# Attention into a mixture of experts on one core: the order of the first two units, identity matmuls in a pause, and W2's buffers

## The chip, the core and the metric

The kernel runs on one core of a Trainium2 chip. Its engines each have an instruction queue of their own: PE (TensorE, matmuls), PEld (its weight loads), DVE (VectorE), ACT (ScalarE), POOL (GpSimd) and SP (SyncE, whose queue issues nearly all DMAs). The metric is device time of one execution in microseconds. Working memory is SBUF; matmuls write to PSUM, of which the kernel uses four double buffers, all called `dbl`.

## What is computed

Eight batches of 576 tokens and eight heads of 64 columns go through two attentions: 32 summary queries `p` per head attend to k and v, and the tokens `q` attend to the result. The tokens' output then goes through four experts with the weights of `domain_probs`. Shapes: q, k, v 8x8x576x64, p 8x8x32x64, w1 4x512x1024, w2 4x1024x512, all float32.

```python
def _attn_ref(q, k, v, p):
    scale = 1.0 / np.sqrt(q.shape[-1])
    def sm_attn(qq, kk, vv):
        s = scale * np.matmul(qq, kk.transpose(0, 1, 3, 2))
        s = s - np.max(s, axis=-1, keepdims=True)
        a = np.exp(s)
        a = a / (np.sum(a, axis=-1, keepdims=True) + 1e-09)
        return np.matmul(a, vv)
    p_packed = sm_attn(p, k, v)
    return sm_attn(q, p_packed, p_packed)

def _moe_ref(x, domain_probs, w1, w2):
    p = domain_probs / (domain_probs.sum(-1, keepdims=True) + 1e-09)
    out = np.zeros((N, D), dtype=np.float32)
    for e in range(E):
        h = np.maximum(x @ w1[e], 0.0)
        out += p[:, e:e + 1] * (h @ w2[e])
    return out
```

## The kernel before

**Units.** The experts' hidden width, 4 x 1024, is cut into eight blocks `ch` of 512. A unit is one block for one batch; the batches come in four pairs (super-blocks `sb`), and the first units are (block 0, batch 0), (block 1, batch 0), (block 1, batch 1), (block 0, batch 1). What follows speaks of units 0 and 1 above all, both of batch 0, and of unit 2, which is the first of batch 1.

**Attention.** `pack_unit` makes the packed summaries `ppbd` for one batch and one group g of four heads. `tok_unit` makes the tokens' probabilities against the 32 summaries: transposes of the scores (`a`), row maximum m2, a-m, exp on ACT, row sum s2, its inverse, a x s, a transpose back (`at`), and a split of `at` into a high part `xh` (ACT cast) and the rest `xl` (POOL subtraction), so that the product of float32 values can be done in three matmuls of a shorter type. `tok_halves` does this for batch 0 in two halves of 288 tokens, c = 0 and 1: `turned`, `shifted`, `normed`.

**First product.** `g_form` multiplies the summaries by W1 (raw tiles `wraw`) into `ghl`, high and low part. `mm1_group(u, kh, c)` multiplies `ghl` by `xh`/`xl` in 24 matmuls of 288 columns, for half kh of the block and half c of the tokens. DVE then applies relu and the token's weight (`pbt`) in one SCALAR_TENSOR_TENSOR. The four results are the quarters a11, a21, a12, a22 of a matrix.

**Second product.** It is done as a seven-product scheme (Strassen and Winograd): operands a11, a12, a22 and s1 to s4 (sums of quarters, tiles `sblk`, `ablk`) against the corresponding t of W2. `s_operand` splits an operand into `st`, high part on ACT, low part on POOL. `t_form` does the same for W2 (raw tiles `rw0`, `rw1`) into `tt`, and forms t1 to t4 by four subtractions. `product(u, i)` is 12 matmuls of 288 columns, in the sequence ORDER = a11, s3, s1, s2, a22, s4, a12; its result is copied or added to `acc`. At the end of a batch pair `combine` adds the accumulators and stores them.

**What sets the order.** The program is recorded by a helper, and a scheduler then places each engine's instructions by their dependences. Wrappers add order edges: `InOrder` (`vq` for DVE, `gq` for POOL) keeps an engine in the order of the program while `.on` is set; `Behind` (`avec`, `cvec`, `bact`, `bpool`) puts an instruction behind the last one that another wrapper noted. `vec` and `vacc` note DVE's operand sums and accumulations. So all of DVE's and POOL's instructions made through a wrapper appear in the profile under one line, 68. Background attention for batch 1 is a generator, `back`, two steps of which are taken after each product of unit 0.

Of the kernel before, what the change touches and what calls it, by code (L numbers as in the profile page):

```python
# [16 lines left out]
P = 128  # L17
# [16 lines left out]

ORDER = ["a11", "s3", "s1", "s2", "a22", "s4", "a12"]
NPROD = len(ORDER)


@with_exitstack
def attention_moe(ctx: ExitStack, tc: tile.TileContext, q, k, v, p, dp, w1, w2, out):  # L40
# [262 lines left out]
    def tok_halves(b, new):  # L303
        xs[b] = tuple(xpool.tile([P, NG, 2, HP], F32R, name=f"{n}{b // 2 % 2}") for n in ("xh", "xl"))
        qts = []
        for g in range(NG):
            qts.append(new[g](b, [P, 2, S], "qt"))
            nc.sync.dma_start(out=qts[g], in_=q[b][:, 2 * g:2 * g + 2, :])
        yield
        pss = [  # L310
            scores([b], g, lambda b, pr, hh: ppbd[b % 4][hh * D:(hh + 1) * D, pr, :], {b: qts[g]})[b]
            for g in range(NG)
        ]
        yield
        n = HS // 32
        a2s = [new[g](b, [P, 2 * n, NPK], "a1") for g in range(NG)]
        ats = [new[g](b, [P, S], "at") for g in range(NG)]
        def block(g, c):
            return a2s[g][:, c * n:(c + 1) * n]

        def turned(g, c):
            vq.transpose(out=block(g, c).rearrange("p a n -> p (a n)"), in_=pss[g][:, c, 0:HS])

        def shifted(g, c):
            a2 = block(g, c)
            m2 = small.tile([P, n, 1], F32, name="m2")
            vq.tensor_reduce(out=m2, in_=a2, axis=AX.X, op=ALU.max)
            vq.tensor_tensor(out=a2, in0=a2, in1=m2.broadcast_to([P, n, NPK]), op=ALU.subtract)
            nc.scalar.activation(out=a2, in_=a2, func=AF.Exp, scale=SCALE)

        def normed(g, c):
            a2, ts = block(g, c), slice(c * HS, (c + 1) * HS)
            s2 = small.tile([P, n, 1], F32, name="s2")
            vq.tensor_reduce(out=s2, in_=a2, axis=AX.X, op=ALU.add)
            vq.tensor_scalar_add(s2, s2, 1e-9)
            vq.reciprocal(out=s2, in_=s2)
            vq.tensor_tensor(out=a2, in0=a2, in1=s2.broadcast_to([P, n, NPK]), op=ALU.mult)
            vq.transpose(out=ats[g][:, ts], in_=a2.rearrange("p a n -> p (a n)"))
            xh, xl = (t[:, g, c, 0:HS] for t in xs[b])
            hi_of(xh, ats[g][:, ts], nc.scalar)  # L340
            lo_of(xl, ats[g][:, ts], xh, gq)

        for g in range(NG):
            turned(g, 0)
            shifted(g, 0)
        yield
        normed(0, 0)
        for g in range(NG):
            turned(g, 1)
        normed(1, 0)  # L350
        yield
        for g in range(NG):
            shifted(g, 1)
        yield
        for g in range(NG):
            normed(g, 1)
        yield

    def w1_load(ch):
# [10 lines left out]
    def g_form(bs, ch, raws, late=False):  # L370

        pss, calls = {}, []
        for g in range(NG):
            ps = dbl()
            for hs in range(4):
                pr, hh = 2 * g + hs // 2, hs % 2
                rows = slice(hh * D, (hh + 1) * D)
                for b in bs:
                    pss[g, b] = ps[:, b % 2]
                    c0 = (hs // 2) * 2 * NPK + cols(b, hh).start  # L380
                    calls.append(dict(
                        out=pss[g, b][c0:c0 + NPK, :], lhsT=ppbd[b % 4][rows, pr, :], rhs=raws[pr][rows, :],
                        start=True, stop=True,
                    ))
        together(calls)
        for g in range(NG):
            for b in bs:
                ghl = gpool.tile([P, 2, FC], F32R, name="ghl", bufs=6)
                hi_of(ghl[:, 0, :], pss[g, b], nc.scalar)
                if not late:  # L390
                    lo_of(ghl[:, 1, :], pss[g, b], ghl[:, 0, :], vq)
                gs.setdefault((b, ch), []).append(ghl)
            if not late:
                yield
        if late:
            yield
            for g in range(NG):
                for b in bs:
                    ghl = gs[b, ch][g]
                    lo_of(ghl[:, 1, :], pss[g, b], ghl[:, 0, :], vq)  # L400
            yield

    units = [(0, 0, 0), (0, 1, 0), (0, 1, 1), (0, 0, 1)]
# [6 lines left out]
        pbt[b] = t  # L410

    blocks = {}

    def mm1_group(u, kh, c):
        sb, ch, b = units[u]
# [22 lines left out]
        def add(dst, x, y, op):  # L438
            vec.tensor_tensor(out=dst, in0=x, in1=y, op=op)

        name = f"a{c + 1}{kh + 1}"
        vec.scalar_tensor_tensor(
            out=held(name) if c == kh else psv, in0=psv, scalar=0.0,
            in1=pbt[b][:, ts].rearrange("p (o t) -> p o t", o=1).broadcast_to([P, 2, HS]),
            op0=ALU.max, op1=ALU.mult,
        )
        if name == "a21":
            add(held("s3"), blocks[u, "a11"], psv, ALU.subtract)
            add(psv, psv, blocks[u, "a22"], ALU.add)
            add(held("s2"), psv, blocks[u, "a11"], ALU.subtract)  # L450
            nc.scalar.copy(out=held("s1"), in_=psv)  # L451
            if (u, "a12") in blocks:
                add(held("s4"), blocks[u, "a12"], blocks[u, "s2"], ALU.subtract)
        elif name == "a12":
            if (u, "s2") in blocks:
                add(held("s4"), psv, blocks[u, "s2"], ALU.subtract)
            else:
                blocks[u, "a12"] = psv
            st = hpool.tile([P, 2, 2, HP], F32R, name="stl")[:, :, :, 0:HS]
            hi_of(st[:, 0], psv, nc.scalar)  # L460
            lo_of(st[:, 1], psv, st[:, 0], vec)
            blocks[u, "op", NPROD - 1] = st

# [29 lines left out]
    def raw_tile(shape, name):  # L493
        return wpool.tile(shape, F32, name=name)

    def t_form(ch, first=False):

        raw = [w2r.pop((ch, kh)) for kh in range(2)]
        blk = {
# [4 lines left out]
        steps = (  # L504
            ("a11", "t1", "t3"), ("s3", "s1", "t2"), ("s2", "t4"), ("a22",), ("s4",), ("a12",),
        )
        how = {"t1": ("b12", "b11", "b11"), "t2": ("b22", "t1", "t1"), "t3": ("b22", "b12", "b12"), "t4": ("t2", "b21", "t2")}
        for names in steps:
            for name in names:
# [5 lines left out]
            for name in names:  # L515
                if name in how:
                    x, y, place = how[name]
                    bpool.tensor_tensor(out=blk[place], in0=blk[x], in1=blk[y], op=ALU.subtract)
                    blk[name] = blk[place]
                else:  # L520
                    t = tt[ch, ORDER.index(name)]
                    lo_of(t[:, 1], blk[of[name]], t[:, 0], bpool)
# [116 lines left out]
    with ExitStack() as first:  # L639
# [42 lines left out]
            next(gen)  # L682
        next(halves)
        drain(fold)
        next(halves)
        next(forms)
        mm1_group(0, 0, 0)
        s_operand(0, 0)
        next(halves)
        mm1_group(0, 1, 0)  # L690
        for gen in packs[2:]:
            next(gen)
        mm1_group(0, 1, 1)
        mm1_group(0, 0, 1)
        s_operand(0, 1)
        vq.on = gq.on = False
        drain(forms)

    apool = ctx.enter_context(tc.tile_pool(name="apool", bufs=2, reuse_waits="tile"))
# [13 lines left out]
    GROUPS = {1: ((0, 0),), 3: ((1, 1),), 4: ((0, 1),), 6: ((1, 0),)}  # L713
    GROUPS_FIRST = {2: ((0, 0),), 3: ((1, 1),), 4: ((0, 1),), 6: ((1, 0),)}
    GROUPS_LATE = {3: ((0, 0),), 4: ((1, 1),), 5: ((0, 1),), 6: ((1, 0),)}
    FORM = {0: (0, 2, 3, 4, 5, 6), 2: (6,), 3: (0, 1, 2, 3, 4)}
    for kh in range(2):
        w2_load(1, kh, raw_tile)
    tsteps = nothing
    kind = None  # L720
    sums, back = nothing, second_batch()
    for u, (sb, ch, b) in enumerate(units):
        pos = u % (2 * NCH)
        odd = pos % 2 == 1
        opening = u < 4
        nxt = units[u + 1] if u + 1 < len(units) else None

        if u == 1:
            drain(back)
            avec.on = cvec.on = bact.on = bpool.on = order["strict"] = True  # L730
        if sb + 1 < SB and pos == (2 if sb == 0 else 1):
            drain(back)
            back, kind = pair_attention([2 * sb + 2, 2 * sb + 3]), None
# [1 line left out]
        gsteps, gat = nothing, (0, 1)  # L735
        nsb, nch = (sb, ch + 1) if ch + 1 < NCH else (sb + 1, 0)
        if u == 0:
            gsteps, gat = g_form([0], 1, raws), (0,)
        elif u == 1:
            gsteps, gat = g_form([1], 1, raws), (0,)  # L740
        elif u == 2:
            gsteps, gat = g_form([1], 0, raws), (0,)
        elif u > 2 and not odd and nsb < SB:
            gsteps = g_form([2 * nsb, 2 * nsb + 1], nch, raws)
        fch = {0: 1, 2: 2, 3: 2}.get(u, ch + 1 if u > 3 and sb == 0 and ch + 1 < NCH else None)
        if fch is not None and u != 3 and not (u > 3 and odd):
            tsteps = t_form(fch)
        form_at = FORM.get(u, () if fch is None else (1, 2, 3, 4) if odd else (1, 4))
        for i in range(NPROD):
            product(u, i)  # L750
# [3 lines left out]
            elif nxt:  # L754
                s_operand(u + 1, n - NPROD)
            if i in gat:
                if gat == (0,):
                    drain(gsteps)
                    if 0 < u < 4:
                        raws = w1_load({1: 0, 2: 2}[u])  # L760
# [6 lines left out]
                    mm1_group(u + 1, *grp)  # L767
            if i == 4 and 2 <= u < len(units) - 2 and units[u + 2][1] % 2 == 0:
                load_probs(units[u + 2][2], units[u + 2][1] // 2)
            if u == 0:  # L770
                next(back, None)
                next(back, None)
            elif i == 5 and kind != "scores" or i == 2 and u > 2 or i == 0 and odd and u > 3:
                kind = next(back, None)
            if i in form_at:
                next(tsteps, None)
            if u == 1 and i < 2:
                w2_load(2, i, raw_tile)
# [51 lines left out]
```

## Time and profile before

| | before |
|---|---|
| median of 3 runs | 1281.56 us (1281.49 to 1284.88) |
| profiled execution | 1281.34 us, span 1279.6 us |
| mean granted TensorE clock | 0.995 |
| PE busy | 1245.8 us, 97% of the span |
| DVE, ACT, POOL busy | 934.1, 498.2, 734.8 us |
| chain that ended last | PE 90%, DVE 4%, DMA 2%, POOL 2% |

The rows of the timeline read: start in us, duration, engine, line of the program, operation, output tile <- input tiles, shapes, count; the bracket at the end is the idle time of the engine just before, and the instruction that ended it. `[5.68 <-POOL xl L68]` on a PE row means that PE stood still for 5.68 us until POOL had written `xl`. Rows of the waits read: engine and tile, what it waited for, total us, times, longest. Instructions follow each other slightly sooner than their durations say, since the next begins while the last one drains.

### The profile page before, as it was taken

What the parts mean: (1) busy time and instruction counts of PE and PEld (TensorE: products, weight loads), DVE (VectorE), ACT (ScalarE), POOL (GpSimd) and SP (SyncE); (2) the same over time, 40 slices, a digit from 0 to 9 for tenths busy, and PEclk for the clock granted to TensorE, in tenths of its full rate; (3) what the DMA queues carried; (4) which work ended last, traced back from release to release, by engine and by line L of the source; (5) the groups of instructions that cost most, each with busy time, mean ns of one, the idle gap of its engine ahead of it and who ended that gap; (6) DMA issues with size and microseconds to landing.
All of it is one profiled execution on the core that took longest, in us unless ns stands there. A gap on an engine that the chain in (4) does not pass through costs nothing.

```text
span 1279.6 us, 26886 instructions
## 1 busy us (share of the span) xinstructions
PE 1245.8 (97%) x10720; PEld 1165.0 (91%) x10720; DVE 934.1 (73%) x1398; ACT 498.2 (39%) x850; POOL 734.8 (57%) x528
## 2 busy tenths in 40 slices
PE   6899999999999999999999999999999999999996
PEld 3789899999999999999998999999999999999996
DVE  6676676888875677889776667788968466776667
ACT  3554544444445333334325434233334523332331
POOL 3876978798674434455566434454448544544554
PEclk9999999999999999999999999999999999999999
DMA  9765565545556444464444465433346443434322
GB/s 340 253 249 191 208 234 197 193 142 170 182 181 223 155 164 150 140 195 158 136 161 157 158 206 176 152 116 127 118 158 213 154 134 119 132 116 155 125 66 75
DMA packets 86219, 213.71 MB, mean 167 GB/s; under 512 B 8784, under 2 KB 27344, under 8 KB 86096
## 3 DMA queue, kind: packets, MB, share of 16 engines
q1 hardware_dynamic: 85424, 211.85, 49.6%
q8 instruction: 86, 1.41, 0.5%
q14 instruction: 37, 0.30, 0.1%
q10 hardware_dynamic: 672, 0.15, 0.1%
HBM read 173.09 MB, written 38.87 MB: 166 GB/s over the span
## 4 chain that ended last, share of the span: by engine, by line
PE 90%; DVE 4%; DMA 2%; POOL 2%; ACT 1%; issue 1%; DVEq 0%; SPq 0%; POOLq 0%; ACTq 0%
PE dbl L116 84%; PE dbl L124 5%; DVE acc L68 2%; DMA pnd<-ablk 1%; POOL st L68 1%; PE dbl L119 1%; DMA pbt<-pnd 1%; DVE a L68 1%; DVE sblk L68 0%; POOL tt L68 0%; DMA wraw<-in_w 0%; DVE dbl L68 0%; DVE ghl L68 0%; DMA rw<-in_w 0%; ACT st L151 0%
## 5 line engine op out<-in xcount | busy, mean ns | idle before, releaser
L116 PE MATMUL dbl<-st,tt 128*128 128x288 f32 x4608 | 666.4, 296 | 8.9 <-DVE ghl L68 5.1
L116 PEld LDWEIGHTS dbl<-st,tt 128*128 128x128 f32 x4608 | 623.1, 188 | 44.8 <-POOL st L68 24.8
L68 POOL TENSOR_TENSOR st<-sblk,st 128x576 fp32r<-128x576 f32 x256 | 370.0, 1456 | 447.4 <-ACT st L151 446.1
L116 PE MATMUL dbl<-xh,ghl 128*128 128x288 f32 x2048 | 413.6, 294 | 0.0
L68 DVE TENSOR_TENSOR acc<-dbl,acc 128x576 f32<-128x576 f32 x391 | 293.5, 752 | 87.9 <-PE dbl L116 85.5
L116 PEld LDWEIGHTS dbl<-xh,ghl 128*128 128x128 f32 x2048 | 328.2, 188 | 0.2 <-DVE ghl L68 0.2
L151 ACT CAST st<-sblk 128x576 fp32r<-128x576 f32 x256 | 166.7, 675 | 368.6 <-DVE sblk L68 296.7
L116 PE MATMUL dbl<-xl,ghl 128*128 128x288 f32 x1024 | 302.9, 296 | 6.0 <-POOL xl L68 5.7
L68 POOL TENSOR_TENSOR st<-ablk,st 128x576 fp32r<-128x576 f32 x128 | 188.6, 1473 | 45.4 <-ACT st L151 45.3
L116 PEld LDWEIGHTS dbl<-xl,ghl 128*128 128x128 f32 x1024 | 192.7, 188 | 8.8 <-POOL xl L68 6.4
L68 DVE SCALAR_TENSOR_TENSOR dbl<-dbl,pbt 128x576 f32<-128x576 f32 x128 | 97.8, 764 | 80.4 <-PE dbl L116 79.2
L68 DVE SCALAR_TENSOR_TENSOR ablk<-dbl,pbt 128x576 f32<-128x576 f32 x128 | 96.4, 753 | 67.7 <-PE dbl L116 65.2
L151 ACT CAST st<-ablk 128x576 fp32r<-128x576 f32 x128 | 86.3, 674 | 126.7 <-PE dbl L116 93.8
L116 PE MATMUL dbl<-stl,tt 128*128 128x288 f32 x768 | 113.0, 296 | 0.0
L116 PEld LDWEIGHTS dbl<-stl,tt 128*128 128x128 f32 x768 | 104.4, 188 | 0.2
L68 DVE TENSOR_TENSOR ghl<-dbl,ghl 128x512 fp32r<-128x512 f32 x128 | 84.9, 685 | 23.6 <-ACT ghl L151 23.6
L151 ACT CAST ghl<-dbl 128x512 fp32r<-128x512 f32 x128 | 72.3, 590 | 55.8 <-DVE ghl L68 54.8
L68 POOL TENSOR_TENSOR tt<-rw,tt 128x512 fp32r<-128x512 f32 x56 | 72.7, 1315 | 18.6 <-ACT tt L85 18.6
L68 DVE TENSOR_TENSOR stl<-dbl,stl 128x576 fp32r<-128x576 f32 x64 | 48.4, 756 | 39.1 <-ACT stl L151 39.1
L124 PE MATMUL dbl<-wraw,ppbd 64*32 64x512 f32 x1024 | 67.6, 595 | 0.9 <-DMA wraw<-in_w 0.9
L451 ACT COPY sblk<-dbl 128x576 f32<-128x576 f32 x64 | 41.1, 642 | 65.6 <-DVE sblk L68 65.6
L544 ACT COPY acc<-dbl 128x576 f32<-128x576 f32 x56 | 35.9, 642 | 51.8 <-PE dbl L116 49.1
(63 smaller groups left out, 703.4 us busy)
## 6 DMA issues: line engine op xcount, KB each, us to landing
tt<-td SPq DMA_DIRECT2D x175, 512.0 KB, 4.1
wraw<-in_w SPq DMA_DIRECT2D x132, 256.0 KB, 4.3
td<-tt SPq DMA_DIRECT2D x56, 512.0 KB, 5.2
pbt<-pnd SPq DMA_DIRECT2D x32, 288.0 KB, 3.8
out<-acc SPq DMA_DIRECT2D x32, 288.0 KB, 2.7
rw<-in_w SPq DMA_DIRECT2D x16, 512.0 KB, 5.7
kt<-in_k SPq DMA_DIRECT2D x14, 576.0 KB, 5.6
kt<-in_q SPq DMA_DIRECT2D x14, 576.0 KB, 5.4
```

The lines of the kernel that those rows point to most:

```text
L68: res = getattr(self.eng, op)(*args, **kw)
L116: on_pe(nc.tensor.matmul(**kw))
L119: on_pe(nc.tensor.transpose(**kw))
L124: ins = nc.tensor.matmul(**kw).ins
L151: return eng.copy(out=dst, in_=src)
L451: nc.scalar.copy(out=held("s1"), in_=psv)
L544: nc.scalar.copy(out=accs[b, i], in_=psv)
```

## The change

It moves work in the first 90 us and, with it, the places of some later instructions:

- In `tok_halves` the normalisation of the second half's group 0 comes a step sooner; DVE does it ahead of a11's SCALAR_TENSOR_TENSOR.
- `warm(16)` issues 16 matmuls of `ident` with itself, between the first-half and the second-half groups of unit 0.
- a12 of unit 0 is held in SBUF and split as the other operands are, by ACT and POOL (`early`), instead of from PSUM by ACT and DVE (`stl`).
- The operands 1 to 3 of unit 0 are formed in a loop at once, POOL's `gq` stays in order through unit 0, and the wrappers' `on` flags are set before unit 0, not before unit 1.
- In unit 0 `t_form(1)` makes its subtractions by `avec` (DVE), not by `bpool` (POOL), at other positions (FORM); `g_form` follows product 1, not product 0; of `back`, two steps follow each of the first five products of unit 0 and the first two of unit 1.
- Block 1's W2 goes into two buffers of `xpool` named `xh1`, not into `rw0` and `rw1`.
- `g_form`'s low parts are made through `vec`.

```diff
@@ tok_halves
         for g in range(NG):
             shifted(g, 1)
+        normed(0, 1)
         yield
-        for g in range(NG):
-            normed(g, 1)
+        normed(1, 1)
         yield
@@ g_form (twice)
-                    lo_of(ghl[:, 1, :], pss[g, b], ghl[:, 0, :], vq)
+                    lo_of(ghl[:, 1, :], pss[g, b], ghl[:, 0, :], vec)
@@ new
+    def warm(n):
+        ps = dbl()
+        together([
+            dict(out=ps[:, 0, 0:P], lhsT=ident, rhs=ident, start=True, stop=True) for _ in range(n)
+        ])
@@ mm1_group
+        early = name == "a12" and (u, "a22") not in blocks
         vec.scalar_tensor_tensor(
-            out=held(name) if c == kh else psv, in0=psv, scalar=0.0,
+            out=held(name) if c == kh or early else psv, in0=psv, scalar=0.0,
...
-            else:
-                blocks[u, "a12"] = psv
+            if early:
+                return
             st = hpool.tile([P, 2, 2, HP], F32R, name="stl")[:, :, :, 0:HS]
@@ t_form
-    def t_form(ch, first=False):
+    def t_form(ch, first=False, eng=bpool):
...
+        if first:
+            steps = steps[:1] + (("s3", "s1"), ("t2",)) + steps[2:]
...
-                    bpool.tensor_tensor(out=blk[place], in0=blk[x], in1=blk[y], op=ALU.subtract)
+                    eng.tensor_tensor(out=blk[place], in0=blk[x], in1=blk[y], op=ALU.subtract)
@@ the opening
         drain(fold)
+        next(forms)
         next(halves)
         next(forms)
         mm1_group(0, 0, 0)
+        next(halves)
         s_operand(0, 0)
-        next(halves)
         mm1_group(0, 1, 0)
+        next(forms)
+        warm(WARM)
         for gen in packs[2:]:
             next(gen)
         mm1_group(0, 1, 1)
         mm1_group(0, 0, 1)
-        s_operand(0, 1)
-        vq.on = gq.on = False
+        for i in range(1, 4):
+            s_operand(0, i)
+        avec.on = cvec.on = bact.on = bpool.on = order["strict"] = True
+        order["product"] = order["free"][-1]
+        vq.on = False
         drain(forms)
@@ the units
-    FORM = {0: (0, 2, 3, 4, 5, 6), 2: (6,), 3: (0, 1, 2, 3, 4)}
+    FORM = {0: (3, 3, 4, 5, 6, 6), 2: (6,), 3: (0, 1, 2, 3, 4)}
     for kh in range(2):
-        w2_load(1, kh, raw_tile)
+        w2_load(1, kh, lambda shape, name: xpool.tile(shape, F32, name="xh1"))
...
+        gq.on = u == 0
-        if u == 1:
-            drain(back)
-            avec.on = cvec.on = bact.on = bpool.on = order["strict"] = True
...
-            gsteps, gat = g_form([0], 1, raws), (0,)
+            gsteps, gat = g_form([0], 1, raws), (1,)
...
-            tsteps = t_form(fch)
+            tsteps = t_form(fch, eng=bpool if u else avec)
...
-            if u == 0:
-                next(back, None)
-                next(back, None)
+            if u < 2:
+                for _ in range(2 if i < 5 - 3 * u else 0):
+                    next(back, None)
```

In what follows a row gives line, operation, output <- inputs and columns; the number behind a name tells buffers apart.

POOL, from t1 of block 1 to s3 of unit 1. In before `rw0` and `rw1` hold block 1's W2; `st` from sblk_830 is s3, from sblk_835 s1, from sblk_833 s2, from ablk_770 a22, and `xl0` from at_918 is batch 1's.

```order
L68 TENSOR_TENSOR tt_796<-rw0_557,tt_796 128x512
L68 TENSOR_TENSOR rw0_557<-rw0_557,rw1_559 128x2x256
L68 TENSOR_TENSOR tt_845<-rw0_557,tt_845 128x512
L68 TENSOR_TENSOR tt_877<-rw1_559,tt_877 128x512
L68 TENSOR_TENSOR tt_926<-rw1_559,tt_926 128x512
L68 TENSOR_TENSOR st_896<-sblk_830,st_896 128x2x288
L68 TENSOR_TENSOR st_944<-sblk_835,st_944 128x2x288
L68 TENSOR_TENSOR st_988<-sblk_833,st_988 128x2x288
L68 TENSOR_TENSOR st_1008<-ablk_770,st_1008 128x2x288
L68 TENSOR_TENSOR xl0_375<-at_918,xh0_374 128x2x288
```

The same place in after, where `xh1_578` and `xh1_580` hold block 1's W2, ablk_482 is a12 of unit 0, ablk_731 a11 of unit 1, sblk_849 s1, sblk_847 s2 and sblk_844 s3:

```order
L69 TENSOR_TENSOR tt_804<-xh1_578,tt_804 128x512
L69 TENSOR_TENSOR tt_806<-xh1_578,tt_806 128x512
L69 TENSOR_TENSOR st_827<-ablk_482,st_827 128x2x288
L69 TENSOR_TENSOR tt_859<-xh1_578,tt_859 128x512
L69 TENSOR_TENSOR st_879<-ablk_731,st_879 128x2x288
L69 TENSOR_TENSOR st_944<-sblk_849,st_944 128x2x288
L69 TENSOR_TENSOR st_998<-sblk_847,st_998 128x2x288
L69 TENSOR_TENSOR tt_882<-xh1_578,tt_882 128x512
L69 TENSOR_TENSOR st_901<-sblk_844,st_901 128x2x288
```

The subtractions of W2 are gone from POOL, a12's split has come, and s3's (st_901) stands behind s1's and s2's; batch 1's `xl0` follows five instructions later.

DVE, around a21 of unit 1 (dbl_816 in before). a1_781 and a1_793 are the attention tiles of batch 1, one for each head group, m2 and s2 their row maxima and sums.

```order
L68 SCALAR_TENSOR_TENSOR ablk_770<-dbl_757,pbt_313 128x576
L68 STREAM_TRANSPOSE a1_781<-dbl_772 128x288 x2
L68 TENSOR_REDUCE m2_837<-a1_781 128x18
L68 STREAM_TRANSPOSE a1_793<-dbl_784 128x288 x2
L68 TENSOR_TENSOR a1_781<-a1_781,m2_837 128x576
L68 TENSOR_REDUCE m2_841<-a1_793 128x18
L68 TENSOR_TENSOR a1_793<-a1_793,m2_841 128x576
L68 SCALAR_TENSOR_TENSOR dbl_816<-dbl_816,pbt_313 128x2x288
L68 TENSOR_REDUCE s2_867<-a1_781 128x18
```

In after, with dbl_830 for a21 and a1_784 and a1_796 for the attention tiles:

```order
L69 SCALAR_TENSOR_TENSOR ablk_773<-dbl_760,pbt_313 128x576
L69 TENSOR_TENSOR xh1_578<-xh1_578 128x2x256
L69 STREAM_TRANSPOSE a1_784<-dbl_775 128x288 x2
L69 TENSOR_TENSOR xh1_578<-xh1_580,xh1_578 128x2x256
L69 STREAM_TRANSPOSE a1_796<-dbl_787 128x288 x2
L69 SCALAR_TENSOR_TENSOR dbl_830<-dbl_830,pbt_313 128x2x288
L69 TENSOR_TENSOR xh1_578<-xh1_580,xh1_578 128x2x256
L69 TENSOR_TENSOR sblk_844<-ablk_731,dbl_830 128x576
L69 TENSOR_TENSOR dbl_830<-dbl_830,ablk_773 128x2x288
L69 TENSOR_TENSOR sblk_847<-dbl_830,ablk_731 128x576
L69 TENSOR_REDUCE m2_851<-a1_784 128x18
L69 TENSOR_REDUCE m2_855<-a1_796 128x18
```

The maxima and a-m of batch 1 have moved behind a21's product and the sums of quarters, and W2's subtractions have come in between.

DVE at the end of the first super-block, where `combine` (acc_1263, acc_1164 are accumulators) meets `g_form`'s low parts:

```order
L68 TENSOR_TENSOR stl<-dbl,stl 128x2x288
L68 TENSOR_TENSOR acc_1263<-acc_1263,acc_1164 128x576
L68 TENSOR_TENSOR ghl<-dbl,ghl 128x512 x3
L68 SCALAR_TENSOR_TENSOR ablk<-dbl,pbt 128x576
L68 TENSOR_TENSOR acc_1208<-acc_1208,acc_1263 128x576
```

```order
L69 TENSOR_TENSOR stl<-dbl,stl 128x2x288
L69 TENSOR_TENSOR ghl<-dbl,ghl 128x512 x2
L69 TENSOR_TENSOR acc_1281<-acc_1281,acc_1182 128x576
L69 TENSOR_TENSOR ghl<-dbl,ghl 128x512
L69 SCALAR_TENSOR_TENSOR ablk<-dbl,pbt 128x576
```

Two of the three `ghl` now stand ahead of the accumulators' addition. The same holds at the ends of the second and the third super-block.

More of the change, by code (lines that the diff above doesn't have):

```diff
@@ L36 @@
 NPROD = len(ORDER)
+WARM = 16
 @with_exitstack
@@ L399, in g_form @@
                     ghl = gs[b, ch][g]
-                    lo_of(ghl[:, 1, :], pss[g, b], ghl[:, 0, :], vq)
+                    lo_of(ghl[:, 1, :], pss[g, b], ghl[:, 0, :], vec)
             yield
@@ L756, in attention_moe @@
             if i in gat:
-                if gat == (0,):
+                if len(gat) == 1:
                     drain(gsteps)
@@ L769, in attention_moe @@
                 load_probs(units[u + 2][2], units[u + 2][1] // 2)
-            if u == 0:
-                next(back, None)
-                next(back, None)
+            if u < 2:
+                for _ in range(2 if i < 5 - 3 * u else 0):
+                    next(back, None)
             elif i == 5 and kind != "scores" or i == 2 and u > 2 or i == 0 and odd and u > 3:
                 kind = next(back, None)
-            if i in form_at:
+            for _ in range(form_at.count(i)):
                 next(tsteps, None)
```

## The prediction

> **What bounds the kernel now.** I read the page first: one engine is nearly always busy.
>
> ```profile
> PE 1245.8 (97%) x10720; PEld 1165.0 (91%) x10720; DVE 934.1 (73%) x1398; ACT 498.2 (39%) x850; POOL 734.8 (57%) x528
> ```
>
> The span is 1279.6 us, so all that this change can save is in PE's waits, and any new wait of PE is a loss. The view of the waits, for 0 to 80 us and for the rest, ranks them (total, times, longest):
>
> ```profile
> PE dbl L116 <- POOL xl L68: 5.7, 1, 5.7
> ...
> PE dbl L116 <- DVE ghl L68: 5.1, 4, 1.3
> ```
>
> The first is one pause near 30 us; the second is met four times later. The timeline shows the pause:
>
> ```profile
> 26.77 0.46 DVE L68 TENSOR_TENSOR a<-a,m 128x288 f32<-128x288 f32 x1
> 28.16 0.76 DVE L68 SCALAR_TENSOR_TENSOR ablk<-dbl,pbt 128x576 f32<-128x576 f32 x1 [0.94 <-DMA pbt<-pnd]
> 31.29 0.48 DVE L68 STREAM_TRANSPOSE at<-a 128x288 f32<-128x288 f32 x1
> 33.42 0.48 DVE L68 STREAM_TRANSPOSE at<-a 128x288 f32<-128x288 f32 x1
> 34.09 0.61 PE L116 MATMUL dbl<-xl,ghl 128*128 128x288 f32 x1 [5.68 <-POOL xl L68]
> 34.44 0.80 POOL L68 TENSOR_TENSOR xl<-at,xh 128x288 fp32r<-128x288 f32 x1 [0.40 <-ACT xh L151]
> 39.60 1.75 PE L116 MATMUL dbl<-st,tt 128*128 128x288 f32 x12
> ...
> 43.67 1.31 PE L119 MATMUL dbl<-ident,a 128*128 128x128 f32 x10 [0.48 <-ACT sblk L451]
> ```
>
> PE waits 5.68 us because `xh`/`xl` of the second token half do not exist; DVE first does a11's product with the probabilities (28.16), then both heads' normalisation. The view by windows gives the granted clock (us, busy PE, PEld, DVE, ACT, POOL, then PEclk, DMA share, GB/s):
>
> ```profile
> 28.00:30.00 2.00, 0.41 (x4) 0.18 (x2) 1.73 (x5) 0.67 (x1) 1.92 (x3) 1.00 1.02 382
> 30.00:32.00 2.00, 0.00 (x0) 0.00 (x0) 1.97 (x3) 0.20 (x1) 2.00 (x2) 0.82 1.10 369
> 32.00:34.00 2.00, 0.00 (x0) 0.00 (x0) 1.86 (x6) 0.30 (x2) 2.00 (x3) 0.50 1.02 391
> ...
> 38.00:40.00 2.00, 2.00 (x16) 2.00 (x16) 1.29 (x5) 1.62 (x4) 1.32 (x2) 0.98 0.71 289
> ```
>
> PE stopped 0.41 us into the first window, at 28.4. 0.82 means half clock from 31.28 on, 0.98 that it ended near 38.1. The 24 matmuls between 34.09 and 39.60 took 5.51 us.
>
> **The change part by part.** The later boundaries come first, since they stand alone; then I walk both programs along PE, comparing when the same matmuls start.
>
> *The later boundaries.*
>
> ```profile
> 366.78 1.82 DVE L68 TENSOR_TENSOR acc<-acc,acc 128x576 f32<-128x576 f32 x1
> 368.53 0.68 DVE L68 TENSOR_TENSOR ghl<-dbl,ghl 128x512 fp32r<-128x512 f32 x1
> ...
> 370.81 2.47 PE L116 MATMUL dbl<-st,tt 128*128 128x288 f32 x17 [1.29 <-DVE ghl L68]
> ...
> 988.28 3.40 PE L116 MATMUL dbl<-st,tt 128*128 128x288 f32 x24 [1.30 <-DVE ghl L68]
> ```
>
> At three ends of a super-block, of which the first and the last are shown, a 1.82 us addition stands ahead of the `ghl` that PE waits for. In after two `ghl` stand ahead of it; they start 1.75 sooner than at 368.53, more than the 1.29 that PE waited: **-3.9** for three, at worst 0.
>
> *Leg 1, the pause.* DVE now goes from 26.77 straight to g0's normalisation (start 27.2). In before that chain ran from 28.9 to the end of the transpose, 31.77, so 2.9 us: it ends at 30.1 to 30.4 now. Then a11's product, 0.7, to about 31.1; then g1's chain, 2.1 (31.77 to 33.90): 33.3 to 33.8. ACT's cast and POOL's `xl` ended 1.34 behind the transpose in before (35.24 against 33.90): 34.6 to 35.2. The second head's part is needed by the fourth matmul, so 24 matmuls at full clock (0.131 each by the 39.60 row, 1.75 less the last one's 0.30 over 11; 3.15) end at 37.3 to 38.0 against 39.60: 1.6 to 2.3 ahead. a11's own operand follows 2.2 later, with its cast and POOL's part done by 35, still ahead of product(0,0).
>
> The 16 identity matmuls need a free PSUM buffer, which a11's product releases; by the order they start at 31.1, not 28.4. The nearest row is the transposes' against the same `ident`, 0.131 each: 2.1 us, at half clock 4.2. They stand ahead of matmuls that cannot start before 34.2, so only the half-clock end costs anything (up to 1). The nearest row for the clock is before's own: the step down came at 31.28 behind a stretch that held under half a microsecond of PE work. After leaves the same stretch (27.9 to 31.3) nearly as empty: 28.4 to 31.1 is 2.7 us of idleness. The drop therefore can still come, but the identity matmuls fill the next stretch, so it ends about 34.7. I put one such stretch at 0 to 1.7 us (24 matmuls at half clock for part of it), take 0.9, and two at 3.3. [...]
>
> *Leg 2, to 50 us.* The group of 16 `wraw` matmuls moves behind product(0,1), which so comes sooner. But the next lock is the second `at` copy:
>
> ```profile
> 44.74 1.83 PE L116 MATMUL dbl<-st,tt 128*128 128x288 f32 x12
> 47.72 0.74 ACT L85 COPY at<-dbl 128x512 f32<-128x512 f32 x2
> 48.36 0.65 PE L116 MATMUL dbl<-xl,at 128*32 128x64 f32 x32 [0.96 <-ACT at L85]
> ...
> 67.89 1.92 PE L124 MATMUL dbl<-wraw,ppbd 64*32 64x512 f32 x16
> ```
>
> Product(0,1) goes to about 42.5 (44.74). The copy stands behind both `ghl` casts on ACT now, and these wait for the 16 `wraw` matmuls (1.92 for such a group, last row), 42.5 + 1.6 + 1.9 = 46.0; with ACT's queue of some ten casts of about 0.6 ahead of it, it runs at 48.0 and the 48.36 matmuls start at 48.6. The gain is given back: +0.2, taken as level. W2's loads for block 1 move ahead to about 32 us, where the DMA share is already 1.0; ACT's first cast of them comes at 46.5 by this walk, so 14 us cover them, and a delay of 5 us more would still be hidden.
>
> *Leg 3, 50 to 62.* Level: PE has no gap in the window below.
>
> *Leg 4, GpSimd.*
>
> ```profile
> 50.00:60.00 10.00, 10.00 (x93) 8.66 (x92) 4.89 (x12) 3.22 (x6) 9.34 (x8) 1.00 0.34 117
> 53.01 1.30 POOL L68 TENSOR_TENSOR rw<-rw,rw 128x512 f32<-128x512 f32 x1
> 56.30 0.76 DVE L68 SCALAR_TENSOR_TENSOR ablk<-dbl,pbt 128x576 f32<-128x576 f32 x1 [1.86 <-PE dbl L116]
> 64.50 3.80 POOL L68 TENSOR_TENSOR tt<-rw,tt 128x512 fp32r<-128x512 f32 x3 [0.97 <-ACT tt L85]
> 68.25 5.21 POOL L68 TENSOR_TENSOR st<-sblk,st 128x576 fp32r<-128x576 f32 x3
> 71.61 4.98 PE L116 MATMUL dbl<-st,tt 128*128 128x288 f32 x36 [1.81 <-DVE acc L68]
> 74.82 1.43 POOL L68 TENSOR_TENSOR xl<-at,xh 128x576 fp32r<-128x576 f32 x1
> ```
>
> Before, POOL is busy 9.34 of 10 us here; the 53.01 row is one of four subtractions of W2 of 1.30 us. These go to DVE, but by the order DVE does the first behind the 56.30 row (56.9) and the next at 58.2; ACT's casts follow at 58.8 to 59.9. POOL, in order, so idles from 54.1 to 59.5, and the 5.2 us taken off it are lost in that hole. Ahead of `st` of s3 of unit 1 then stand four `tt` (1.27 each by the 64.50 row) and five `st` of 576 columns (1.43 undisturbed as the 74.82 row, 1.74 in the 68.25 row), itself the last: the a12 operand is new on POOL, and s1, s2 and one `tt`, needed later, jump the queue. 59.5 + 4 x 1.25 + 5 x 1.40 (start to start) = 71.5, plus 1.9 for waits on DVE's later two subtractions and 0.9 for collisions with DVE (three at 0.31, 1.74 less 1.43), gives 74.3; the 1.9 is an estimate of the walk. Product(1,1), the 71.61 row, starts 2.7 later.
>
> *Leg 5, attention of batch 1.*
>
> ```profile
> 59.68 0.72 DVE L68 TENSOR_TENSOR a<-a,m 128x576 f32<-128x576 f32 x1
> 60.32 0.74 DVE L68 TENSOR_REDUCE m<-a 128x18 f32<-128x576 f32 x1
> 61.09 1.27 DVE L68 TENSOR_TENSOR a<-a,m 128x576 f32<-128x576 f32 x1
> 62.29 0.75 DVE L68 SCALAR_TENSOR_TENSOR dbl<-dbl,pbt 128x576 f32<-128x576 f32 x1
> 67.99 0.92 DVE L68 TENSOR_TENSOR a<-a,s 128x576 f32<-128x576 f32 x1
> 69.50 1.30 DVE L68 TENSOR_TENSOR a<-a,s 128x576 f32<-128x576 f32 x1
> 71.39 0.76 DVE L68 STREAM_TRANSPOSE at<-a 128x576 f32<-128x576 f32 x1
> 76.43 0.30 PE L116 MATMUL dbl<-xl,ghl 128*128 128x288 f32 x1
> 77.30 0.77 DVE L68 STREAM_TRANSPOSE at<-a 128x576 f32<-128x576 f32 x1
> 78.86 1.44 POOL L68 TENSOR_TENSOR xl<-at,xh 128x576 fp32r<-128x576 f32 x1 [1.22 <-ACT xh L85]
> ```
>
> From the 62.29 product to the `at` transpose DVE takes 9.10 us without a gap. After puts ten more instructions in between, for they once stood ahead of this stretch or behind it: two reductions m2, two `ghl`, `stl` and one accumulation, 0.66 each (0.74, of which 0.08 lies under the next: 59.68 + 0.72 against 60.32), 4.0; and four that read both inputs from SBUF, two a-m and two W2 subtractions. These four are the open price: 0.64 alone (59.68 to 60.32), 1.20 beside a busy POOL (61.09 to 62.29), 1.75 at most (366.78 to 368.53). POOL has no hole from 59.5 to 74.3, so I take 1.45, between the second and the third. 62.29 + 9.10 + 4.0 + 5.8 = 81.2; transpose to `xl` 1.56 (77.30 to 78.86), `xl` 1.43, to PE 0.18 (74.82 + 1.43 to 76.43): 84.3 where 76.43 was, **+7.8**. The ends are +4.7 (0.64) and +10.5 (1.75, the a x s products included, which at 67.99 and 69.50 took 0.84 and 1.2 to the next). Leg 4's 2.7 lies inside this, since PE waits here anyway. Behind it PE has no gap, so the loss stays.
>
> [...]
>
> **Sum.** The profiled execution took 1281.34, 0.22 under the median of 1281.56. 1281.34 + 7.8 + 0.9 - 3.9 = 1286.1.
>
> **Rivals.** 0.3%, 3.84 us, is what a measurement of this kernel can tell from no change: slower is above 1285.4, faster below 1277.7.
> 1. The four DVE operations miss POOL and run at 0.64: +4.7 for leg 5, 1283.0. For: 59.68 did, beside a running POOL. Against: 61.09 and 69.50.
> 2. The clock holds through the pause: 1285.2. For: the gap is half of before's. Against: the 28 to 30 window.
> 3. The clock stays at half for both stretches: 3.3 in place of 0.9, 1288.5. For: the start of the identity matmuls is late.
> 4. Batch 1's attention is not late: PE's own in-order work is what ends at 76.4, leg 1's gain of 2.0 is kept, and the boundaries give 3.9: 1281.34 - 5.9 = 1275.4, faster. It decides if `at` is transposed by 73.3 (76.43 less 3.17). For: leg 4's POOL is relieved of 5.2 us. Against: DVE's ten extra instructions need at least 6.6 us.
> 5. All four two-input operations, and the a x s products, collide in full: +10.5, 1288.8. For: the 366.78 row and POOL without a hole. Against: 59.68 and 67.99 did not.
> 6. The DVE order at the boundaries brings nothing: 1290.0. Against: PE's releaser there is named three times.
>
> **Numbers.** The forecast has 0.38 (1286.1), rival 1 0.20, rival 2 0.15, rival 3 0.07, rival 4 0.10, rival 5 0.06, rival 6 0.04. Slower than 1285.4: 0.27 of the forecast (its own range is 1284 to 1288.5), half of rival 2, rivals 3, 5 and 6 whole, 0.02 of rival 1: 0.52. Faster: rival 4 and 0.01 of rival 1. The rest, 0.37, is within 0.3%. The range, 1280.5 to 1289.5, holds the bounds of leg 5 (1283.0 and 1288.8) with some room for the walk's error below, and leaves out rivals 4 and 6.
>
> **What would show it.** Leg 1: PE's `xl` wait near 28 to 34 shrinks, the groups end by 38. Leg 2: the matmuls of the second `at` start within 0.5 of 48.4. Leg 4: a POOL hole of 4 to 6 us near 54 to 59, and PE waiting for `st` about 3 us near 71. Leg 5: a PE wait on POOL `xl` of 4 to 6 us ending near 84, with a-m or a x s rows above 1.2. Boundaries: no `ghl` waits of 1.3. The prediction is wrong if the `xl` of batch 1 is there by 78, or if the loss by 100 us is under 5.

## The result and the profile after

The changed kernel takes 1290.7 us (median of 4, 1290.31 to 1291.07) where the kernel before takes 1282.15 (1281.49 to 1284.88) beside it: 1.0063 times as long, interval 1.0045 to 1.008. It is slower, as forecast, but by 8.6 us and not by 4.8, and it lies above the range. The profiled execution has a span of 1288.9 us against 1279.6, so 9.3 us more.

The page's first line and the waits of PE, up to 100 us and behind (total, times, longest):

```profile
PE 1252.6 (97%) x10752; PEld 1173.1 (91%) x10752; DVE 937.6 (73%) x1401; ACT 497.7 (39%) x850; POOL 730.8 (57%) x525
```

```profile
PE dbl L117 <- POOL st L69: 6.1, 4, 3.4
...
PE dbl L117 <- POOL xl L69: 3.5, 1, 3.5
PE dbl L125 <- DVE ablk L69: 2.7, 1, 2.7
PE dbl L117 <- ACT at L86: 1.6, 1, 1.6
...
PE dbl L117 <- DVE ghl L69: 2.0, 1, 2.0
```

There are 32 more PE instructions, not 16. The 5.68 wait in the pause has gone; what replaced it are `st` (6.1 in four waits, the longest of them leg 4), a later `xl` (leg 5) and the identity matmuls' own wait of 2.7. Three of the four later waits for `ghl` are gone. The timeline of the pause:

```profile
30.52 0.72 DVE L69 SCALAR_TENSOR_TENSOR ablk<-dbl,pbt 128x576 f32<-128x576 f32 x1
31.29 6.78 PE L125 MATMUL dbl<-ident 128*128 128x128 f32 x32 [2.71 <-DVE ablk L69]
33.51 0.48 DVE L69 STREAM_TRANSPOSE at<-a 128x288 f32<-128x288 f32 x1
34.53 0.79 POOL L69 TENSOR_TENSOR xl<-at,xh 128x288 fp32r<-128x288 f32 x1 [1.37 <-ACT xh L152]
37.83 0.38 PE L117 MATMUL dbl<-xl,ghl 128*128 128x288 f32 x1
41.08 1.74 PE L117 MATMUL dbl<-st,tt 128*128 128x288 f32 x12
```

`xl` is there at 35.3, but PE is in the identity matmuls until 37.83: each float32 matmul appears in the trace as two PE instructions (passes, from here on), 32 in all, at 0.204 us (6.54 over 32). The clock, by windows (us, PE, PEld, DVE, ACT, POOL, PEclk, DMA share, GB/s):

```profile
28.00:30.00 2.00, 0.58 (x5) 0.35 (x3) 1.93 (x3) 0.00 (x0) 1.76 (x2) 1.00 1.03 387
30.00:32.00 2.00, 0.71 (x3) 0.71 (x4) 1.90 (x6) 1.10 (x2) 0.86 (x2) 0.67 1.08 369
...
36.00:38.00 2.00, 2.00 (x13) 2.00 (x13) 0.30 (x2) 1.25 (x4) 1.92 (x3) 0.63 1.03 383
...
88.00:90.00 2.00, 2.00 (x11) 2.00 (x12) 0.69 (x1) 0.67 (x1) 0.52 (x1) 0.67 0.00 0
90.00:92.00 2.00, 2.00 (x10) 2.00 (x9) 0.66 (x1) 0.00 (x0) 0.88 (x1) 0.50 0.00 0
92.00:94.00 2.00, 2.00 (x17) 2.00 (x16) 0.36 (x2) 0.00 (x0) 0.00 (x0) 0.97 0.00 0
```

0.67 and 0.63 put the half clock from 30.68 to 37.48, 6.8 us, over nearly all the identity matmuls. It comes again from 88.7 to 92.1, behind leg 5's wait. The timeline of legs 2, 4 and 5:

```profile
51.70 0.90 PE L117 MATMUL dbl<-xl,at 128*32 128x64 f32 x40 [1.57 <-ACT at L86]
62.88 2.54 POOL L69 TENSOR_TENSOR tt<-xh,tt 128x512 fp32r<-128x512 f32 x2 [5.65 <-ACT tt L86]
64.83 0.77 DVE L69 SCALAR_TENSOR_TENSOR dbl<-dbl,pbt 128x576 f32<-128x576 f32 x1 [1.93 <-PE dbl L117]
65.50 1.84 DVE L69 TENSOR_TENSOR xh<-xh,xh 128x512 f32<-128x512 f32 x1
70.72 0.68 DVE L69 TENSOR_TENSOR xh<-xh,xh 128x512 f32<-128x512 f32 x1
71.31 2.66 DVE L69 TENSOR_TENSOR a<-a,m 128x576 f32<-128x576 f32 x2
77.89 2.32 PE L117 MATMUL dbl<-st,tt 128*128 128x288 f32 x10 [3.38 <-POOL st L69]
79.07 2.64 DVE L69 TENSOR_SCALAR s<-s 128x18 f32<-128x18 f32 x2
84.94 0.76 DVE L69 STREAM_TRANSPOSE at<-a 128x576 f32<-128x576 f32 x1
87.94 0.40 PE L117 MATMUL dbl<-xl,ghl 128*128 128x288 f32 x1 [3.50 <-POOL xl L69]
```

The same matmuls stood at 48.36, 71.61 and 76.43 before, so after is 3.3 late in leg 2, 6.3 in leg 4 and 11.5 in leg 5. POOL's hole is there (5.65 us ahead of 62.88). The end of the first super-block, and a wait of PE at 150.79 for `ghl` that was 1.22 in before:

```profile
150.79 1.81 PE L117 MATMUL dbl<-st,tt 128*128 128x288 f32 x12 [2.03 <-DVE ghl L69]
...
381.78 0.69 DVE L69 TENSOR_TENSOR ghl<-dbl,ghl 128x512 fp32r<-128x512 f32 x1 [0.65 <-ACT ghl L152]
382.38 1.31 DVE L69 TENSOR_TENSOR acc<-acc,acc 128x576 f32<-128x576 f32 x1
383.02 2.27 PE L117 MATMUL dbl<-st,tt 128*128 128x288 f32 x16
```

The matmul of 383.02, 370.81 in before, waits for nothing now.

### The profile page after: what moved, and what is told of

The parts are those of the page before. It is cut to its first block, busy times and chain, and to the rows that moved or that the text cites. A ratio compares the mean times of both kernels' runs of the same rounds, so it can differ in the third digit from the quotient of the medians.

```text
span 1288.9 us, 26949 instructions
## 1 busy us (share of the span) xinstructions
PE 1252.6 (97%) x10752; PEld 1173.1 (91%) x10752; DVE 937.6 (73%) x1401; ACT 497.7 (39%) x850; POOL 730.8 (57%) x525
## 4 chain that ended last, share of the span: by engine, by line
PE 91%; DVE 5%; POOL 2%; ACT 1%; issue 1%; DMA 0%; DVEq 0%; SPq 0%; ACTq 0%; POOLq 0%
PE dbl L117 84%; PE dbl L125 6%; DVE acc L69 1%; DVE a L69 1%; POOL st L69 1%; PE dbl L120 1%; DVE s L69 1%; DVE dbl L69 0%; DVE sblk L69 0%; POOL tt L69 0%; DMA kt<-in_k 0%; DVE ghl L69 0%; DVE m L69 0%; POOL rw L69 0%; POOL acc L69 0%
## 5 line engine op out<-in xcount | busy, mean ns | idle before, releaser
L69 POOL TENSOR_TENSOR tt<-rw,tt 128x512 fp32r<-128x512 f32 x49 | 63.8, 1320 | 16.6 <-ACT tt L86 16.4
```

The costliest lines, as they stand in the source:

```text
L69: res = getattr(self.eng, op)(*args, **kw)
```

## The experiments

**One identity matmul instead of 16 (n1).**

```diff
-WARM = 16
+WARM = 1
```

> The changed kernel with 1 identity matmul in place of 16 (they are issued as 32 passes in the trace and held PE from 31.29 to 37.83). Theory A, their own price pushed everything behind them: the second-half groups start near 35.0, end 2 to 3 us sooner than 41.08, and the kernel takes about 1288. Theory B, the half clock and ACT's queue set leg 2 whatever PE does in the pause: PE idles from 28.6 to about 35, runs at half clock until about 37.5, ends the groups at 39.5 to 40.5, the second at copy is within 1 us of 51.1, and the kernel takes 1289.5 to 1291.

Measured 1288.23 (1287.57 to 1289.13), 2.5 below the changed kernel. The second-half groups end at 38.90, not 41.08. Theory A fits: the identity matmuls' own time is what the leg paid; without 15 of them the half clock (6.83 us here as well) costs the groups less.

**Identity transposes, one pass each, instead of identity matmuls (tr16).**

```diff
-        together([
-            dict(out=ps[:, 0, 0:P], lhsT=ident, rhs=ident, start=True, stop=True) for _ in range(n)
-        ])
+        for i in range(n):
+            ins = nc.tensor.transpose(out=ps[:, 0, 0:P], in_=ident, identity=ident).ins
...
```

> The changed kernel with 16 identity transposes in place of the 16 identity matmuls: one pass each by the rows of the transposes (0.11 to 0.13 us at full clock) and not two. If the passes' time is what delayed the second-half groups, 16 passes at half clock end near 34.9, ahead of xl, and it takes what one identity matmul takes, 1288.2, give or take 0.8. Rival, PE in use in the pause is itself harmful or helps the clock: off by over 1.5 from that.

Measured 1287.46 (1287.01 to 1288.74). The PE row of its pause, and that of the next experiment, in which the clock happened to stay at 1.00:

```profile
31.91 3.63 PE L419 MATMUL dbl<-ident 128*128 128x128 f32 x16 [2.71 <-DVE ablk L69]
35.40 0.37 PE L117 MATMUL dbl<-xl,ghl 128*128 128x288 f32 x1
```

```profile
31.46 3.84 PE L125 MATMUL dbl<-ident 128*128 128x128 f32 x32 [2.72 <-DVE ablk L69]
35.06 0.38 PE L117 MATMUL dbl<-xl,ghl 128*128 128x288 f32 x1
```

A pass is 0.218 at half clock in the first (3.49 over 16) and 0.113 at full clock in the second. So 16 matmuls are 3.6 us at full clock and 6.5 at half; 16 transposes fit into the pause either way. The time is 0.7 below the 1288.2 expected, so the theory of the passes fits, and PE's use in the pause is not harmful in itself. The 3.2 us between the two kernels need not be the second pass alone: in this execution the half clock lasted one stretch (31.95 to 35.36), in the changed kernel's two. n1, with two stretches as well, gives 2.5.

**Batch 1's attention stepped as before (back).**

```diff
-            if u < 2:
-                for _ in range(2 if i < 5 - 3 * u else 0):
-                    next(back, None)
+            if u == 0:
+                next(back, None)
+                next(back, None)
...
+        if u == 1:
+            drain(back)
```

> The changed kernel with batch 1's attention stepped as before (two steps after each product of unit 0, the rest drained ahead of unit 1); all else as changed. If leg 5 of the prediction holds (the attention's place on DVE makes xl late), the 3.5 us wait for xl near 88 goes to 0 to 1.5 and the kernel takes 1287 to 1289. Rival, POOL's order (leg 4) sets it: the wait for st of s3 stays at 3.4, xl stays late, 1290 to 1291.

Measured 1287.55 (1286.82 to 1288.77), 3.1 below. PE's wait for batch 1's `xl` goes from 3.5 to 0.8 (at 87.06), as leg 5 expects; a wait of 3.4 for DVE's `s` stands where leg 4's for `st` was (76.78). In the profiled execution the clock also stayed up in the pause (1.00 from 28 to 40 us), so some of the 3.1 may not be the steps'.

```profile
87.06 0.40 PE L117 MATMUL dbl<-xl,ghl 128*128 128x288 f32 x1 [0.83 <-POOL xl L69]
```

**The steps, and the order edges too, as before (flags1_back).** On top of the edit above:

```diff
-        avec.on = cvec.on = bact.on = bpool.on = order["strict"] = True
-        order["product"] = order["free"][-1]
         vq.on = False
...
         if u == 1:
             drain(back)
+            avec.on = cvec.on = bact.on = bpool.on = order["strict"] = True
```

> The changed kernel with both parts that move batch 1's attention undone: the order edges come into force at unit 1, and attention is stepped and drained as before. If leg 5 is that move, xl's wait near 88 goes and 4 to 6 us come back, 1285 to 1286.5, with leg 4's wait for st of s3 left. Rival, POOL's order holds xl back as much: 1288 or more.

Measured 1285.38 (1283.31 to 1287.53): 5.3 of the 8.6 come back, and no wait for batch 1's `xl` is left. Leg 5 is the place of batch 1's attention, and the edges have a part in it. Leg 4's wait for `st` of s3, which was to stay, is gone too: PE waits 2.75 for DVE's `acc` there (77.83).

**The subtractions of block 1's W2 on POOL again (form).**

```diff
-            tsteps = t_form(fch, eng=bpool if u else avec)
+            tsteps = t_form(fch)
```

> The changed kernel with t_form's four subtractions of block 1 back on POOL. Leg 5 as written counts two of them at 1.45 in DVE's stretch ahead of at: xl comes 2.9 sooner, 1287.8. Rival, POOL in order is as full as DVE: with 5.2 us more work it ends its xl as late, the wait only changes its place, and it takes 1290 to 1292.

Measured 1286.79 (1286.31 to 1291.73), 3.9 below. DVE's stretch in its timeline:

```profile
63.48 0.77 DVE L69 SCALAR_TENSOR_TENSOR dbl<-dbl,pbt 128x576 f32<-128x576 f32 x1 [2.48 <-PE dbl L117]
...
69.54 1.31 DVE L69 TENSOR_TENSOR a<-a,m 128x576 f32<-128x576 f32 x1
...
81.09 0.77 DVE L69 STREAM_TRANSPOSE at<-a 128x576 f32<-128x576 f32 x1
```

17.6 us against 20.1 (64.83 to 84.94) in the changed kernel: 2.5, near the 2.9 expected; the other 1.35 (63.48 for 64.83) came earlier, in an execution whose clock stayed up in the pause (1.00 from 28 to 40 us). POOL, with 5.2 us more work, does not hold `xl` back, because the subtractions fill the hole that it had ahead of 62.88. So moving them to DVE cost DVE and did not free POOL. Leg 4's wait is nearly gone as well (0.51 for 3.38), which is why PE, though it goes on 3.85 sooner (84.09 for 87.94), now waits longer for `xl`, 5.99.

**The `ghl` order alone, on the kernel before (ghl).**

```diff
-                    lo_of(ghl[:, 1, :], pss[g, b], ghl[:, 0, :], vq)
+                    lo_of(ghl[:, 1, :], pss[g, b], ghl[:, 0, :], vec)
```

(both places)

> The kernel before with g_form's low parts made through vec, nothing else: only the order of ghl and acc<-acc,acc on DVE at three ends of a super-block changes. The prediction's term: three waits of 1.29 go, 1281.5 - 3.9 = 1277.6. What the changed kernel's trace shows there (shifts of -1.76, -1.54, -1.54 between equal matmuls): -4.8, 1276.7. Rival, the gain belongs to the rest of the change: 1281.5.

Measured 1277.82 (1277.39 to 1277.99) against 1282.37 beside it: ratio 0.9963, 0.995 to 0.9975. Its PE row at the first boundary has no wait:

```profile
369.27 0.69 DVE L68 TENSOR_TENSOR ghl<-dbl,ghl 128x512 fp32r<-128x512 f32 x1 [0.66 <-ACT ghl L151]
369.88 1.29 DVE L68 TENSOR_TENSOR acc<-acc,acc 128x576 f32<-128x576 f32 x1
...
370.51 3.32 PE L116 MATMUL dbl<-st,tt 128*128 128x288 f32 x24
```

It is faster than both kernels, and these two lines are the only part of the change tried here that gained.

**Identity matmuls that start earlier, on the ghl kernel (ghl_w24).** `warm(24)` behind the same group, with the second half's normalisation left in its old place, so that a11's product comes first on DVE.

> The kernel before with the ghl edit and 24 identity matmuls in the pause, where a11's product comes first on DVE, so that they start near 29.0 and not at 31.3. If a clock stretch that is half busy holds the clock, no half clock near 31 to 38, the 24 matmuls of the second half take 3.2 us and not 5.5, and it takes 2 us less than the ghl kernel, about 1275. Rival, the clock drops anyway: 48 passes at 0.2 us end near 38.8, the groups start 4.5 us late, about 1279 to 1281.

Measured 1279.37 (1277.01 to 1282.51): not faster than ghl on the median. In its profiled execution, the slowest of the nine, the clock held:

```profile
28.90 5.62 PE L124 MATMUL dbl<-ident 128*128 128x128 f32 x48 [0.40 <-DVE ablk L68]
34.67 0.37 PE L116 MATMUL dbl<-xl,ghl 128*128 128x288 f32 x1
```

```profile
32.00:34.00 2.00, 2.00 (x20) 2.00 (x19) 1.86 (x6) 0.33 (x1) 2.00 (x3) 1.00 1.03 390
...
74.00:76.00 2.00, 2.00 (x11) 2.00 (x10) 1.83 (x4) 0.64 (x2) 2.00 (x2) 0.54 1.01 397
```

Yet the second half's other group waits 1.0 for a PSUM buffer that ACT frees, so the faster clock finds the next lock (product(0,0) starts at 39.59, in before at 39.60); and that execution dropped to half clock at 74 and 142 instead, for 3.4 us each. The median lies in the rival's range, but in this execution not by the rival's way, since the clock did not drop in the pause. So in this execution the clock was held (1.00 from 28 to 38 us), and on the median the kernel gains nothing; what the faster executions did is not recorded.

**The order edges alone, on the ghl kernel (flags).** `avec`, `cvec`, `bact`, `bpool` on ahead of unit 0.

> The ghl kernel with one thing more of the change: the order edges that keep attention, accumulations and W2's forming behind the operand sums (avec, cvec, bact, bpool) are in force from unit 0 and not from unit 1; attention is stepped as before, W2 formed on POOL, no identity matmuls. If the place of batch 1's attention on DVE is what makes xl late (leg 5), these edges alone bring it: a wait of PE for xl or at near 76 to 88 of 5 us or more, 1285 to 1290. Rival, leg 5 comes from the SBUF collisions or from POOL's queue of the changed kernel: under 1280.

Measured 1294.88 (1293.75 to 1296.36), 17.1 above ghl and outside both expectations. It doesn't answer its question: another wait came up. ACT's and POOL's rows:

```profile
71.63 0.62 ACT L85 CAST tt<-rw 128x512 fp32r<-128x512 f32 x1 [8.12 <-DMA rw<-in_w]
```

```profile
72.33 1.26 POOL L68 TENSOR_TENSOR tt<-rw,tt 128x512 fp32r<-128x512 f32 x1 [11.12 <-ACT tt L85]
```

The edges hold back the last uses of block 0's W2, so block 1's, in the same two buffers, is loaded later (issued at 61.21, in ghl at 41.72), and ACT stands before its cast with everything else behind. The changed kernel has the same edges and buffers of their own for block 1, and no such wait; that the buffers are what spares it was not tried by itself.

**Those buffers alone, on the ghl kernel (ghl_xh).**

```diff
-        w2_load(1, kh, raw_tile)
+        w2_load(1, kh, lambda shape, name: xpool.tile(shape, F32, name="xh1"))
```

> The ghl kernel with block 1's W2 in the two xh1 buffers and nothing else of the change. The prediction counts this at nothing, its loads being hidden: 1277.8. Rival, the earlier arrival lets W2's casts and subtractions go ahead of operands on ACT and POOL, which have no order edges there, and displaces them: 1279 to 1281.

Measured 1280.13 (1279.23 to 1282.79), 2.3 above ghl. The loads are hidden, but the order is not indifferent: W2's work and attention fall into other places on DVE and POOL. In both kernels the second a x s stands ahead of the `ghl` that PE needs, but here it meets POOL's `xl` (73.10 to 74.54) and takes 2.02, not 1.29, and the `ghl` come 1.8 later. The rows of ghl, then those of this kernel:

```profile
70.67 1.29 DVE L68 TENSOR_TENSOR a<-a,s 128x576 f32<-128x576 f32 x1
73.24 0.65 DVE L68 TENSOR_TENSOR ghl<-dbl,ghl 128x512 fp32r<-128x512 f32 x1
```

```profile
73.12 2.02 DVE L68 TENSOR_TENSOR a<-a,s 128x576 f32<-128x576 f32 x1
75.07 1.27 DVE L68 TENSOR_TENSOR ghl<-dbl,ghl 128x512 fp32r<-128x512 f32 x2
75.89 3.27 PE L116 MATMUL dbl<-st,tt 128*128 128x288 f32 x23 [1.39 <-DVE ghl L68]
```

Of the two profiled executions this one is level with ghl at 72.69 (72.78), 1.5 behind at 81.50 (79.96) and 2.7 behind at 140.61 (137.94), where PE's wait for `ghl` is 2.31 and not 1.19; why that later wait grew was not followed.

**Three parts undone at once (undo3):** the edits of tr16, form and flags1_back together.

> The changed kernel with three parts undone at once: identity transposes for identity matmuls (alone: 1287.5 against 1290.7), W2's subtractions back on POOL (alone 1286.8), order edges and attention steps of batch 1 as before (alone 1285.4). If the three losses are separate, 1290.7 - 3.2 - 3.9 - 5.3 = 1278.3, beside the ghl kernel. Rival, they overlap (all three delay the same wait of PE for xl), and the new places of the second half and of POOL's rows keep a loss of their own: 1281 to 1283.

Measured 1282.83 (1282.01 to 1287.07): the losses overlap, 7.9 come back and not 12.4. Against ghl 5.0 are still lost, 2.3 of it what the W2 buffers cost alone; the rest, by its list of waits, goes in the main to PSUM buffers that ACT and DVE free late (2.9 and 2.4, in ghl 0 and 1.8). How it divides between the second half's new place and POOL's was not tried.

## Why the prediction was right in sign and wrong in size

- *The pause (leg 1): the step that failed.* The identity matmuls were priced by the row of the transposes, 0.131, as 2.1 us, 4.2 at half clock, hidden or nearly. They took 6.54. The row was of another kind of instruction: in these traces a transpose is one pass (x16 for 16 in tr16), a float32 matmul two (x32 for 16 in after), and the prediction's own rows could have told it (the 67.89 row has x16 for the eight `wraw` matmuls that `g_form` issues for one batch). n1 and tr16 give the price of a term that was put at up to 1: 2.5 and 3.2. The DVE chain itself went nearly as worked out (`at` at 33.99, `xl` at 35.3, each 0.1 to 0.2 behind its range).
- *The clock* was to fall for one stretch, 0.9, taken between 0 and 1.7; that it would end near 34.7 was the author's estimate. It fell for two, 30.68 to 37.50, as rival 3 had it, and later for two more that had no term: the one at 88.7 costs 1.64 where PE is the bound (11.51 late at 87.94, 13.15 at 93.53, which was 80.38). In tr16 it was 3.41 us, 31.95 to 35.36. The drop came here at a gap of 2.71, as the row of before suggested; but back and form, with gaps of 2.72 and 2.7, kept the clock at 1.00. What decides between the two is not shown, and the drop in the profiled execution may be in part chance.
- *Leg 2.* "The gain is given back, +0.2": with transposes it is so, nearly (49.19 for 48.36, +0.8, after a lead of 1.0 at product(0,0), 38.63 for 39.60). With the identity matmuls it became +3.3, and what follows inherits most of it (64.83 for 62.29, 2.5, where leg 5 starts on DVE).
- *Leg 4* was right: 2.7 forecast, 6.3 less 3.3 measured, with POOL's hole of 5.65 us where it was said to be.
- *Leg 5* was right in place and nearly in size: +7.8 forecast (its own terms add up to 84.37, so 7.9), 11.5 less 3.3, 8.2, measured. DVE's stretch took 20.1 where 18.9 were forecast. The nearness is partly luck: the four two-input operations took less (1.77, 0.59, 0.67 and 1.91, sum 4.9, forecast 5.8), and the two TENSOR_SCALAR of 18 columns, not foreseen, 1.3 each in place of about 0.4. The row of 2.66 for the two a-m hides two lengths; one by one, with POOL's rows beside them:

```profile
65.38 1.42 POOL L69 TENSOR_TENSOR st<-ablk,st 128x576 fp32r<-128x576 f32 x1
69.33 1.42 POOL L69 TENSOR_TENSOR st<-ablk,st 128x576 fp32r<-128x576 f32 x1
71.31 0.75 DVE L69 TENSOR_TENSOR a<-a,m 128x576 f32<-128x576 f32 x1
71.35 2.01 POOL L69 TENSOR_TENSOR st<-sblk,st 128x576 fp32r<-128x576 f32 x1 [0.60 <-ACT st L152]
71.98 1.99 DVE L69 TENSOR_TENSOR a<-a,m 128x576 f32<-128x576 f32 x1
```

  The operation of 65.50 ends at 67.34, 0.54 behind POOL's of 65.38 (66.80), and that of 71.98 ends at 73.97, 0.61 behind POOL's of 71.35 (73.36): by these times each ended about as long behind POOL's as such an operation takes alone (0.59 for that of 70.72). That of 70.72 ran in POOL's hole ahead of 71.35, and that of 71.31 was there first; POOL's of 71.35 took 2.01 and not 1.42. What failed in rival 5 is that all four would meet a POOL instruction, since POOL had holes (1.28 ahead of 68.08, 0.60 ahead of 71.35); and rival 1, that none would, is out too. Its witness, the 59.68 row of before, did not run beside POOL for long: POOL's subtraction of 58.42 was done at 59.72.
- *W2's early load* was counted at nothing, on the ground that it is hidden. Alone it costs 2.3, by the new places of DVE's and POOL's work; some of that may lie in the wait at 150.79 (140.61 in ghl_xh), which grew in both.
- *The boundaries* were forecast at -3.9 and gave -4.8 (PE 13.97 late at 150.79, 9.13 at 988.28's matmul), and -4.5 alone in ghl.

The terms: 3.3 in legs 1 and 2, which the sum took as level, 0.4 more in leg 5, 1.6 for the stretch at 88.7, 0.8 for the longer wait at 150.79, less 0.9 that the clock's term had held and 0.9 at the boundaries, is 4.3 of the 4.5 that the spans differ from the forecast. (The parts of the chance of slower add up to 0.535, not to 0.52.)

## What to carry to other kernels

Price an added instruction by a row of the same kind and type, and count the passes that its kind leaves in the trace: filler that must hold an engine for 2 us and holds it for 6.5 is itself the wait. Filler for a clock is worth its place only if the next lock behind it is not already waiting for something else, as it was in ghl_w24. When a change of many parts loses, run its smallest part alone: here two words of an order edge were worth 4.5 us, and no other part that was tried gained anything.

## What the runs showed of the hardware

Up to the idle end of the kernel the half clock lasted 6.82 us in before (31.28 to 38.10); 6.83, 3.41 and 3.41 in after (from 30.68, 78.44 and 88.70); and 10.24 in ghl (30.42 to 40.66). In the 3.41 us ahead of each drop, as long as the shortest of these stretches, PE was in work for 0.54 us in before, and for 1.31, 0.55 and 0.76 in after. In after the clock was at half until 37.50 though PE was in work from 31.29 on. In tr16 it was at half from 31.95 to 35.36, a stretch in which PE ran nothing but the transposes, and at full behind it.

Gaps of the same length went with different clocks. In after the half clock began within a gap of 2.71 (28.58 to 31.29); in back the pause has a gap of 2.72 (28.74 to 31.46), so that the 3.41 us that end with it hold 0.69 us of PE work at most, and the clock stayed at 1.00. A gap of 1.57 ahead of 51.70 in after left the clock at 1.00, with 1.84 us of PE work in the 3.41 us up to 51.70. In back a gap of the same length ended at 49.05, PE had 1.84 us of work in the 3.41 us up to 50.25, and there the clock fell:

```profile
50.00:52.00 2.00, 2.00 (x10) 2.00 (x11) 0.28 (x1) 0.00 (x0) 2.00 (x3) 0.56 0.93 193
```

So neither the gap nor PE's time in work in those 3.41 us told by itself whether the clock fell: it stayed with 0.69 at most and fell with 1.84, more than half of the 3.41. That a stretch half busy holds the clock, the condition in the expectation of ghl_w24, was an assumption and does not hold there. Why some kernels scatter (ghl_w24 from 1277.01 at a granted clock of 0.998 to 1282.51 at 0.995, flags1_back from 1283.31 at 0.995 to 1287.53 at 0.992) and the ghl kernel hardly does (1277.39 to 1277.99), though its clock falls too, is not shown.
